# An attention block on one core: a transposed tile ahead of the whole score tile, and VectorE instead of ScalarE copying the V bank

## The chip, the cores and the metric

The kernel runs on one core of one Trainium2 chip. The core's engines work on their own instruction queues and wait for one another through semaphores: TensorE (matmuls; in the profile PE, and PEld for its weight loads), VectorE (DVE), ScalarE (ACT), GpSimd (POOL) and SyncE (SP, which here issues transfers). Matmul results lie in eight PSUM banks of 128 partitions x 512 floats; TensorE writes them, VectorE and ScalarE read them.

The metric is the device time of one execution in microseconds: 1590.65 (median of 3 runs).

## What is computed

```python
def _A_ref(x, wqkv, wo):                      # 2048 rows, D = 512, H = 32 heads of 16
    qkv = (x @ wqkv).reshape(B, S, 3, H, Dh).transpose(2, 0, 3, 1, 4)
    q, k, v = qkv[0], qkv[1], qkv[2]
    scores = jnp.einsum("bhqd,bhkd->bhqk", q, k) * (Dh ** -0.5)
    p = _softmax(scores, axis=-1)
    o = jnp.einsum("bhqk,bhkd->bhqd", p, v)
    return o.transpose(0, 2, 1, 3).reshape(B, S, D) @ wo
...
xn = _layernorm(x, axis=-1)
s = _A_ref(xn, A_wqkv, A_wo)
g = _silu(_B_ref(xn, B_w1, B_b1, B_w2, B_b2))     # gelu MLP, 512 -> 1376 -> 512
return x + s * g
```

With 32 heads of 16 columns each, there are 32 x 2048 x 2048 = 134 million scores, and as many exponentials.

## The kernel before, in words

The work falls into a first part (layer norm, the projections, the MLP, with score maxima mixed in), a long attention stage, and a tail that multiplies with `wo`, applies the gate and stores. The change touches the attention stage.

**Units and steps.** Four heads (a group `g`) and 512 queries (`c`) make a unit `u`; there are `NU` = 32 units. A unit takes 16 steps, one for each 128 keys. The loop over steps is in lines 966 to 984, and what a step issues, in which order, is a string of letters in `ORDER` (line 40):

- `T` (`t_one`, line 732): a transposed score tile, 128 keys x 512 queries of one head, one matmul (line 739) into a bank, and on ScalarE the exponential of it into SBUF (line 741). Four per step, one per head. The first two are on row side 1 of the matmul array (partitions 64 and up), the last two on row side 0. Four banks go round (`t_tile`, line 724), so a T takes the bank of the T four before it, and must wait for that one's exponential.
- `S` (line 210): a score tile the other way round, 128 queries x 512 keys, only for the row maximum that the softmax subtracts: one matmul (line 183) and on VectorE one `tensor_reduce` (line 189). The first S of a step is on row side 0, the second on side 1. This runs ahead of the T by up to `LEAD` = 144 steps.
- `X` and `Y` (lines 216 to 232): 256 keys of one head on side 0 and the same 256 keys of another head on side 1, in the two halves of one bank, with one reduce after Y. A step thus has three reduces. The S, X and Y tiles use three banks in a ring (`s_ring`). By the order in which the ring gives them out, the first S of a step takes the bank of the first S of the step before, X that of the second S, and the second S that of the X and Y.
- `V` (`pv_step`, line 798): the products with V for the step before, four matmuls in four column tiles into the one V bank, accumulated over a unit's 16 steps. (The trace shows each as two, so a V group has eight rows.) After a unit's last step the bank is copied into `OS[u]` (line 811), after which the next unit's first V matmul may overwrite it.

While score tiles remain to be made, a step is `ORDER[3]`; after step 490 it is `ORDER[0]`, without S, X and Y. Steps 0 and 1 have strings of their own (line 970).

**What hangs on the letters.** Between the T there are slots for other work (`todo`, filled by `at`, line 919): after the i-th T of a step the entries of position i are issued. Position 0 holds `o_move` (line 821: transfers on SP that read `OS[u]`) and `o_den` (line 830: a `reciprocal` on VectorE, then two transfers on SP); all else has position 3. When a unit's score tiles are complete, `s_end0` (line 238) puts one more reduce on VectorE (line 247) behind the next tile's reduce, and for each pair of units a transposing matmul (line 267) and a small copy follow the V of a later step.

Each engine executes its queue in the order of the program; nothing is rescheduled (`manual_schedule`). Two matmuls that stand next to each other on different row sides run side by side.

Of the kernel before, what the change touches and what calls it, by code (L numbers as in the profile page):

```python
# [10 lines left out]
AF = mybir.ActivationFunctionType  # L11
# [25 lines left out]
FILL0 = 30  # L37
HB = 4
W2B = 2
ORDER = {0: "TTTTV", 3: "STXTTSTYV"}  # L40
HC = CH // 2
PAIRED = 28
KB = 3
# [5 lines left out]
def fused(ctx: ExitStack, tc: tile.TileContext, x, wqk, wv, wo, w1, b1, w2, b2, out):  # L49
    nc = tc.nc  # L50
# [746 lines left out]
    PV, OS, DN, DR = {}, {}, {}, {}  # L797
    def pv_step(u, k):
        g = u // NCH
        if k == 0:  # L800
            PV[u] = ps_v.tile([P, CH], F32, name="pv")
        for j in range(GH):
            h = (g * GH + j) * VW
            nc.tensor.matmul(PV[u][32 * j:32 * j + 32, :], vsb[:, k, h:h + 32], PT[u, k][:, j, :],  # L804
                             start=(k == 0), stop=(k == NT - 1))
        del PT[u, k]
        if k == NT - 1:
            OS[u] = wb.tile([P, CH], F32, name="os", bufs=1)
            pv = PV.pop(u)
            if u < NU - 1:  # L810
                nc.scalar.activation(OS[u], pv, AF.Copy)
            else:
                nc.scalar.activation(OS[u][:, :HC], pv[:, :HC], AF.Copy)
                nc.vector.tensor_copy(OS[u][:, HC:], pv[:, HC:])
# [151 lines left out]
    for n in range(L + 1):  # L966
        ua, ka = divmod(n, 16)
        want = due(n) - due(n - 1)
        i = 0
        for op in ORDER[want] if n > 1 else ("TTTTV", "TTSTSVT")[n]:  # L970
            if op in "SXY":
                s_op(op)
            elif op == "V":
                if n:
                    pv_step(*divmod(n - 1, 16))
                for _ in range(4):
                    tick()
                flush()
            else:
                if EARLY <= 4 * n + i < 4 * L:  # L980
                    t_one(ua, ka, i % 2, 1 - i // 2)
                for f, args in todo.get((n, i), []):
                    f(*args)
                i += 1
# [54 lines left out]
```

## Time and profile before

| | us |
|---|---|
| median of 3 runs (1590.64 to 1590.91) | 1590.65 |
| the profiled execution | 1590.04 |
| its span, first to last instruction | 1588.3 |
| TensorE / VectorE / ScalarE busy in the span | 1581.8 / 1379.1 / 1259.1 |
| granted TensorE clock | 1.000 |

The attention stage takes from about 477 to 1499 us of the span. In the timeline, a row gives start, length, engine, line, operation, output and inputs, shape, and in brackets the idle time of the engine ahead of it with what ended it. Rows of one kind that follow one another on an engine are merged and counted with x. Several waits of one instruction are put down to the one that came last. TensorE's matmuls overlap and their ends are modelled, so the starts are what to read.

### The profile page before, as it was taken

The numbers are of one execution on the slowest core, as the hardware profiler recorded it, in microseconds if no ns is written. First come the engines' busy times: TensorE is split into PE (matmuls) and PEld (weight loads), VectorE is DVE, ScalarE is ACT, GpSimd is POOL, SyncE is SP. The second block draws the span as 40 slices with busy tenths as digits, with TensorE's granted clock in tenths as the row PEclk, the third lists the DMA queues.
The fourth block names the chain that finished last, engine by engine and source line by source line (L and its number), as shares of the span: only waits on it lengthen the run. The fifth ranks groups of instructions, "written<-read, shape, count | busy, mean of one in ns | idle before, by whom it ended". The sixth has DMA issues, their size and how long they took to land.

```text
span 1588.3 us, 31761 instructions
## 1 busy us (share of the span) xinstructions
PE 1581.8 (100%) x12144; PEld 934.7 (59%) x12144; DVE 1379.1 (87%) x2261; ACT 1259.1 (79%) x2520; POOL 373.7 (24%) x394
## 2 busy tenths in 40 slices
PE   9999999999999999999999999999999999999998
PEld 8899999999894444444444444444444444444445
DVE  7599898989889999999999999999999999999734
ACT  4334343434349999999999999999999999999984
POOL 4145575756640011001000100100100000000143
PEclk9999999999999999999999999999999999999999
DMA  6626343454332123112410511411150111110252
GB/s 206 150 59 161 109 137 99 157 139 134 114 96 59 37 42 59 28 38 47 76 31 25 70 41 30 62 39 29 33 76 21 32 29 36 36 29 22 59 192 101
DMA packets 74648, 116.87 MB, mean 74 GB/s; under 512 B 23012, under 2 KB 24292, under 8 KB 73320
## 3 DMA queue, kind: packets, MB, share of 16 engines
q1 hardware_dynamic: 70748, 101.89, 23.7%
q0 software_dynamic: 3264, 12.35, 4.5%
q8 instruction: 96, 1.57, 0.4%
q10 hardware_dynamic: 484, 0.60, 0.1%
q14 instruction: 56, 0.46, 0.1%
HBM read 84.35 MB, written 25.97 MB: 69 GB/s over the span
## 4 chain that ended last, share of the span: by engine, by line
PE 97%; ACT 1%; DVE 1%; issue 0%; DMA 0%; ACTq 0%; DVEq 0%
PE pv L804 33%; PE ps L183 24%; PE ps L590 12%; PE pst L739 10%; PE pst L590 7%; PE ps L739 3%; PE ps L80 3%; PE pv L590 2%; PE ps L458 1%; ACT slot L741 1%; PE pst L80 1%; DVE st L417 0%; PE pst L440 0%; DMA xt<-in_x 0%; PE pst L458 0%
## 5 line engine op out<-in xcount | busy, mean ns | idle before, releaser
L189 DVE TENSOR_REDUCE mx<-ps 128x2 f32<-128x512 f32 x2048 | 1299.5, 684 | 144.6 <-PE pst L739 35.2
L741 ACT ACTIVATE slot<-pst 128x512 f32<-128x512 f32 x1533 | 831.7, 614 | 17.8 <-PE pst L739 9.6
L804 PE MATMUL pv<-slot,vsb 128*32 128x512 f32 x4096 | 545.4, 605 | 0.0
L183 PEld LDWEIGHTS ps<-kt,slot 48*128 48x128 f32 x1364 | 223.8, 184 | 280.2 <-DVE mx L189 278.3
L183 PE MATMUL ps<-kt,slot 48*128 48x512 f32 x1364 | 379.4, 365 | 0.0
L739 PE MATMUL pst<-qt,kt 50*128 50x512 f32 x1149 | 376.0, 436 | 0.5 <-DVE gt L672 0.3
L741 ACT ACTIVATE slot<-ps 128x512 f32<-128x512 f32 x515 | 316.5, 615 | 2.5 <-PE ps L183 0.2
L590 PE MATMUL ps<-slot,w1h 64*128 64x512 f32 x1088 | 218.1, 393 | 0.0
L739 PEld LDWEIGHTS pst<-qt,kt 50*128 50x128 f32 x1149 | 188.6, 184 | 41.8 <-ACT slot L865 12.6
L183 PE MATMUL ps<-kt,qz 48*128 48x512 f32 x512 | 212.7, 415 | 0.0
L183 PEld LDWEIGHTS ps<-slot,slot 48*128 48x128 f32 x598 | 98.3, 184 | 121.5 <-DVE mx L189 120.7
L183 PE MATMUL ps<-slot,slot 48*128 48x512 f32 x598 | 166.0, 364 | 0.0
L739 PE MATMUL ps<-qt,kt 50*128 50x512 f32 x387 | 162.7, 422 | 0.0
L590 PEld LDWEIGHTS ps<-slot,w1h 64*128 64x128 f32 x1088 | 151.5, 185 | 8.4 <-ACT junk L604 2.6
L804 PEld LDWEIGHTS pv<-slot,vsb 128*32 128x32 f32 x4096 | 80.8, 108 | 109.2 <-issue 100.2
L590 PE MATMUL ps<-slot,w1l 64*128 64x512 f32 x544 | 141.9, 393 | 0.0
L377 POOL TENSOR_TENSOR hl<-hg,hh 128x512 fp32r<-128x512 f32 x76 | 96.8, 1295 | 129.7 <-ACT hh L376 85.9
L250 POOL CAST nmh<-nm 128x16 fp32r<-128x16 f32 x32 | 6.3, 196 | 477.4 <-DVE nm L247 409.3
L739 PE MATMUL pst<-qt,slot 50*128 50x512 f32 x384 | 113.4, 421 | 0.0
L604 ACT ACTIVATE junk<-ident_r 1x1 f32<-1x1 f32 x92 | 18.0, 196 | 116.5 <-PE pst L590 113.3
L183 PEld LDWEIGHTS ps<-kt,qz 48*128 48x128 f32 x512 | 93.8, 183 | 16.3
L842 POOL TENSOR_TENSOR ot<-ot,dn 64x512 f32<-64x512 f32 x15 | 19.6, 1304 | 299.7 <-DMA dn<-den_d 256.9
(159 smaller groups left out, 1757.7 us busy)
## 6 DMA issues: line engine op xcount, KB each, us to landing
raw<-in_w SPq DMA_DIRECT2D x88, 256.0 KB
qk_h<-hh SPq DMA_DIRECT2D x32, 256.0 KB
qk_l<-hl SPq DMA_DIRECT2D x32, 256.0 KB
qt<-qk_h SPq DMA_DIRECT2D x128, 64.0 KB
slot<-qk_h SPq DMA_DIRECT2D x92, 64.0 KB
g_d<-gt POOLq DMA_DIRECT2D x16, 256.0 KB, 3.5
qt<-qk_l SPq DMA_DIRECT2D x64, 64.0 KB
dn<-den_d SPq DMA_DIRECT2D x32, 128.0 KB
```

The costliest lines, as they stand in the source:

```text
L80: nc.tensor.matmul(ps, lhs[a], rhs[b], start=first and n == 0, stop=last and n == 2)
L183: return nc.tensor.matmul(ps[:, c0:c0 + w], QS[u][r, p, qi * P:(qi + 1) * P], kts[u // NCH % KB][p][r, k0:k0 + w], start=True, stop=True).ins
L189: nc.vector.tensor_reduce(MX[u][:, 2 * p:2 * p + 2, qi, ki][:, heads, parts], ps.rearrange("p (n c) -> p n c", c=HC), axis=AX.X, op=OP.max)
L250: nc.gpsimd.tensor_copy(hl[:, 0], nm)
L377: nc.gpsimd.tensor_sub(hl, raw, hh.bitcast(F32))
L458: nc.tensor.matmul(pq["q", g, c], W1[g][i][:, k * P:(k + 1) * P], (xh, xl)[j][c][:, k], start=n == 0 and k == 0, stop=n == 2 and k == KT - 1)
L590: i = nc.tensor.matmul(ps, lhs[r], rhs[r], start=first, stop=last).ins
L604: i = nc.scalar.activation(junk[:, :1], ident_r[:1, :1].bitcast(F32), AF.Copy).ins
L739: nc.tensor.matmul(ps, kts[g % KB][p][r, k * P:(k + 1) * P], QT[u][r, p, :], start=True, stop=True)
L741: nc.scalar.activation(PT[u, k][:, 2 * p + a, :], ps, AF.Exp, scale=SCALE)
L804: nc.tensor.matmul(PV[u][32 * j:32 * j + 32, :], vsb[:, k, h:h + 32], PT[u, k][:, j, :], start=(k == 0), stop=(k == NT - 1))
L842: eng.tensor_mul(ot[c][rs, g // 2], ot[c][rs, g // 2], DN.pop(u)[rs])
```

## The change

Two lines. The letter string of a full step begins with T instead of S, so that the first transposed tile stands ahead of the first whole score tile. And for all units but the last, the copy of the V bank is issued on VectorE instead of ScalarE.

```diff
-ORDER = {0: "TTTTV", 3: "STXTTSTYV"}
+ORDER = {0: "TTTTV", 3: "TSXTTSTYV"}
...
             if u < NU - 1:
-                nc.scalar.activation(OS[u], pv, AF.Copy)
+                nc.vector.tensor_copy(OS[u], pv)
             else:
```

In the built program, TensorE's queue has the two matmuls exchanged in each of these steps and no others moved; S still waits for VectorE alone and T for ScalarE. The unit's copy is gone from ScalarE's queue and stands on VectorE's behind the last reduce of the unit's last step. The reciprocal of `o_den` moves ahead of the first reduce of its step, since it follows the first T. The queues of GpSimd and SP are unchanged.

## The prediction

> **What bounds the kernel now.** I read the page first, then the busy time by stage.
>
> ```profile
> span 1588.3 us, 31761 instructions
> ...
> PE 97%; ACT 1%; DVE 1%; issue 0%; DMA 0%; ACTq 0%; DVEq 0%
> ```
> ```profile
> 577.81:777.70 199.89, 199.89 (x1540) 90.17 (x1539) 182.95 (x301) 197.98 (x391) 23.98 (x38) 1.00 0.27 50
> 500.00:1498.00 998.00, 998.00 (x7677) 450.06 (x7673) 913.26 (x1501) 988.11 (x1946) 74.59 (x123) 1.00 0.20 40
> 1498.00:1588.30 90.30, 86.27 (x477) 46.01 (x469) 37.03 (x53) 61.63 (x120) 36.26 (x28) 1.00 0.43 143
> ```
>
> The columns are PE, PEld, DVE, ACT, POOL, granted clock, DMA share, GB/s. The changed code runs in this long stage: 490 steps of four exponentials each, (2048 - 576) / 3 from the code. PE is full by its modelled ends, ACT 99%, DVE 92%. Such shares name no owner, so next I measured the step, on the chain of waits, and followed one step in the timeline.
>
> ```profile
> 767.40 1.07 PE pv L804 x8
> ...
> 775.61 1.07 PE pv L804 x8
> ```
> ```profile
> 563.95 0.68 DVE L189 TENSOR_REDUCE mx<-ps 128x2 f32<-128x512 f32 x1
> 564.30 0.50 PE L183 MATMUL ps<-slot,slot 48*128 48x512 f32 x1
> 564.31 0.49 PE L739 MATMUL pst<-qt,kt 50*128 50x512 f32 x1
> 564.87 1.58 ACT L741 ACTIVATE slot<-pst 128x512 f32<-128x512 f32 x3
> 565.32 1.07 PE L804 MATMUL pv<-slot,vsb 128*32 128x512 f32 x8
> 566.32 0.62 ACT L741 ACTIVATE slot<-ps 128x512 f32<-128x512 f32 x1
> 566.99 0.18 PEld L739 LDWEIGHTS ps<-qt,kt 50*128 50x128 f32 x1
> 567.42 0.64 PE L804 MATMUL pv<-slot,vsb 128*32 128x512 f32 x4
> ```
> ```profile
> 564.84 0.69 DVE L189 TENSOR_REDUCE mx<-ps 128x2 f32<-128x512 f32 x1 [0.21 <-PE ps L183]
> ```
> ```profile
> 568.42 0.49 PE L739 MATMUL pst<-qt,kt 50*128 50x512 f32 x1
> ```
>
> Each step ends with a V group. Four steps take 775.61 - 767.40 = 8.21 us, so two take 4.11. A ring of waits gives exactly that. The first T of a step (564.31) is answered by its exponential after 0.56 (564.87); the fourth exponential starts 1.45 later (566.32) and lasts 0.62; 0.05 after its end the fourth T of the *next* step, which needs that bank, loads its weights (566.99); the V group follows 0.43 later (567.42), and the next step's first T 1.00 after it (568.42). Sum 0.56 + 1.45 + 0.62 + 0.05 + 0.43 + 1.00 = 4.11. So the pace is a ring between TensorE and ScalarE over two steps.
>
> The second ring goes over VectorE:
>
> ```profile
> 561.49 1.22 DVE L189 TENSOR_REDUCE mx<-ps 128x2 f32<-128x512 f32 x2
> ```
> ```profile
> 562.76 0.18 PEld L183 LDWEIGHTS ps<-slot,slot 48*128 48x128 f32 x1
> 563.31 0.64 PE L804 MATMUL pv<-slot,vsb 128*32 128x512 f32 x4
> ```
> ```profile
> 608.38 1.89 DVE L189 TENSOR_REDUCE mx<-ps 128x2 f32<-128x512 f32 x3
> 610.47 1.89 DVE L189 TENSOR_REDUCE mx<-ps 128x2 f32<-128x512 f32 x3 [0.21 <-PE pst L739]
> 612.54 0.69 DVE L189 TENSOR_REDUCE mx<-ps 128x2 f32<-128x512 f32 x1 [0.18 <-PE pst L739]
> ```
>
> First S to its reduce 0.54 (564.30 to 564.84); three reduces 1.89; 0.05 from the third's end (562.71) to the weight load of the next step's second S (562.76); 0.55 from there to V; 1.00 to the next S: 4.03. It is 0.08 shorter than the first ring, and so does not show. TensorE alone can do 2.01, as in the step from 563.31 to 565.32, or 4.02 for two. One row misleads:
>
> ```profile
> PEld ps L183 <- DVE mx L189: 386.5, 461, 0.8
> ```
>
> TensorE's largest wait names VectorE. But the first S comes 1.00 after every V group, and T starts 0.01 after it: these 0.84 us are V's own streaming, during which no weights are loaded.
>
> **The swap of S and T.** Nothing is added; T starts 0.01 earlier at most. What differs is who is answered first. With S first, S's reduce starts 0.54 after S, T's exponential 0.56 to 0.57 after T. Before and behind the stage there are steps in which T comes first:
>
> ```profile
> 478.50 0.49 PE L739 MATMUL pst<-qt,kt 50*128 50x512 f32 x1
> ...
> 479.03 0.60 ACT L741 ACTIVATE slot<-pst 128x512 f32<-128x512 f32 x1 [0.83 <-PE ps L739]
> ```
> ```profile
> 1507.91 0.73 PE L739 MATMUL pst<-qt,kt 50*128 50x512 f32 x3
> ...
> 1508.45 1.57 ACT L741 ACTIVATE slot<-pst 128x512 f32<-128x512 f32 x3 [1.18 <-PE pst L739]
> ```
>
> There the exponential comes after 0.53 and 0.54. So the first of the pair is answered about 0.03 sooner, on either engine, and the second pays it. The swap takes 0.03 off the first ring (4.08) and puts 0.03 on the second (4.06); TensorE's own 4.02 lies below both. A unit of 16 steps has eight pairs; at its end the ring is broken by the stall described next, so seven or eight pairs count: 30.6 units x 7.5 x 0.03 = **6.9 us gained**. Bounds: 0, if T second is no cause, and 30.6 x 8 x 0.04 = 9.8, with 0.04 as the most that the rounded rows allow.
>
> The Trainium skill (TensorE: Matmul & The Clock Gate, "The cost: per-tile semaphore tail") says that the completion signals of matmuls running side by side are written one after another, 26.3 ns each. By that figure the term is an estimated 6.0 us, and the rule speaks against the swap as well: the delay isn't removed, S's reduces inherit it. The trace's 0.03 agrees.
>
> Two small things follow on VectorE. The reciprocal of line 832 is issued in the slot after the first T, so it now stands ahead of the step's first reduce, in idle time of 0.21, instead of between two reduces; and line 247's reduce finds a spare of 0.02 in the second ring where it found 0.08.
>
> ```profile
> L832 DVE RECIPROCAL dr<-dr 128x16 f32<-128x16 f32 x29 | 7.0, 242 | 0.0
> L247 DVE TENSOR_REDUCE nm<-mx 128x16 f32<-128x128 f32 x22 | 6.1, 275 | 0.0
> ```
>
> I take +0.02 x 29 = 0.6 gained (0 to 0.05 each) and 0.04 x 22 = 0.9 lost (0 to 0.06 each): **0.3 lost**. The SP and POOL queues keep their order; line 826's transfers wait for a copy that ends no later (below).
>
> **The copy.** Around a unit's end:
>
> ```profile
> 608.94 1.07 PE L804 MATMUL pv<-slot,vsb 128*32 128x512 f32 x8
> 609.93 0.50 PE L183 MATMUL ps<-kt,slot 48*128 48x512 f32 x1
> 610.33 0.63 ACT L811 ACTIVATE os<-pv 128x512 f32<-128x512 f32 x1
> 611.02 0.16 PEld L804 LDWEIGHTS pv<-slot,vsb 128*32 128x32 f32 x8 [0.23 <-ACT os L811]
> 612.24 0.69 ACT L741 ACTIVATE slot<-ps 128x512 f32<-128x512 f32 x1
> 612.98 0.18 PEld L739 LDWEIGHTS ps<-qt,kt 50*128 50x128 f32 x1 [0.30 <-ACT slot L741]
> 613.40 1.07 PE L804 MATMUL pv<-slot,vsb 128*32 128x512 f32 x8
> ```
>
> *Removed*: ScalarE's copy at 610.33 pushes the four exponentials back; the fourth ends 612.93, the T that needs its bank loads at 612.98, and the two steps take 613.40 - 608.94 = 4.46 instead of 4.11. That is 0.35 per unit, 10.5 us over the 30 units that end in this stage (a 31st ends behind it, where VectorE is busy 37 of 90 us, and I count nothing).
>
> *Added*: a copy on VectorE behind the third reduce of the unit's last step. No full copy of this bank on VectorE is in the trace; the nearest rows are its half and other readers of these banks:
>
> ```profile
> L814 DVE COPY os<-pv x1: 424/424/424, 1567.8 to 1567.8; 128x256 f32<-128x256 f32 x1
> L672 DVE TENSOR_TENSOR gt<-pv,b_sb x1: 692/692/692, 475.1 to 475.1; 128x512 f32<-128x512 f32 x1
> ```
>
> I take 0.69 long, and a slot of 0.60 in the queue, as the reduces have: (1.89 - 0.69) / 2. The third reduce starts at 608.38 + 2 x 0.60 = 609.58, with the swap 609.61. The copy runs from 610.21 (V ended at 610.01) to 610.90, and the V group, due at 609.93 + 1.02 = 610.95, finds its bank free; where steps are 0.05 shorter it is 0.05 late. Behind the copy wait the next three reduces: the first starts at 610.81 instead of 610.50, the third ends 612.70, the second S loads at 612.75, and V comes at 613.30 instead of 610.95 + 2.04 = 612.99. So VectorE stalls TensorE by 0.31 to 0.36 where ScalarE did by 0.35: nearly the whole gain is handed back. With 0.34 it is 30 x 0.01 = **0.3 us gained**. Ends: with 0.42, the half's length, as slot the stall is 0.16, gain 5.7; with a slot of 0.69, 0.43, loss 2.4.
>
> The Trainium skill (VectorE: DVE Perf Modes, "The DRAIN you can't avoid") holds that a VectorE instruction starts only when the pipe is empty, which gives the slot of 0.69. The reduces disagree: 0.60 from start to start though 0.69 long.
>
> **Sum.** 6.9 - 0.3 + 0.3 = 6.9 off the profiled execution's 1590.04 (its span 1588.3 and 1.7 around it): 1583.1. The median of the runs is 0.6 above that execution: **1583.8**.
>
> **The rivals.**
> - *The copy costs nothing.* If the slot is short and its lateness dies in VectorE's idle 0.21, the full 10.5 of the removed stall comes on top of the swap's: 1573.6. For it: VectorE is 92% busy. Against: the chain of 613.30 above. A partial case (slot 0.42) is 1578.4.
> - *The swap does nothing.* The two matmuls start 0.01 apart, and if 0.56 against 0.53 belongs to what surrounds those steps, only the copy's 0.3 is left: 1590.4, no change. For it: only steps of other make-up have T first. Against: S, when first, is answered after the same 0.54 on another engine.
> - *VectorE becomes the bound, and the kernel slower.* It decides once the first S's reduce starts 0.62 or more after S: then the second ring is 4.11 or longer. At 0.64 it is 4.13: 240 pairs x 0.02 = 4.8; line 247's slots come through, 22 x 0.08 = 1.8; each copy stalls 0.06 more than ScalarE's did, 1.8: 1599.0. For it: only 0.02 lies between the rings after the change. Against: the second of the pair is now answered within 0.57.
> - *The copy holds VectorE for its whole length*: 30 x 0.09 = 2.7 lost, 1586.5. Its basis is the page's rule above; the reduces speak against it.
>
> **How the numbers follow.** Forecast 0.50 (its own range 1580 to 1587.5); copy free or nearly 0.13; swap without effect 0.17; VectorE the bound 0.14; whole length 0.06. About 0.2% (3.2 us) is what a measurement of this kernel can tell from no change. Faster by more: 0.50 + 0.13 + 0.06, less 0.02 for the forecast's upper edge, 0.67; same 0.18; slower 0.15. The range takes in the forecast, the swap without effect, the partial copy and the whole length: 1576.5 to 1592.5.
>
> **What would show it.** Right: the first exponential 0.53 to 0.54 behind a step's first T, the first reduce 0.57 behind S; pairs of V groups 4.08 apart; at a unit's end a copy of some 0.69 on VectorE, then a V group about 0.3 late, with the second S's weight load 0.05 behind a reduce. Wrong: pairs still 4.11 apart (swap without effect), every second S loading 0.05 behind the third reduce (VectorE paces), or unit ends without a late V group.

## The result and the profile after

| | us |
|---|---|
| before, median of 6 runs beside it | 1590.64 |
| after, median of 6 runs (1580.57 to 1581.35) | 1580.92 |
| ratio, 95% interval | 0.9939, 0.9926 to 0.9952 |
| span of the profiled execution, before and after | 1588.3, 1579.0 |

The kernel became 9.7 us faster; 6.9 was forecast. Two lines of the page of the changed kernel, its span and the chain that ended last by engine, and TensorE's two longest waits between 500 and 1490 us (us in total, times, longest):

```profile
span 1579.0 us, 31736 instructions
...
PE 98%; DVE 1%; DMA 0%; issue 0%; ACT 0%; DVEq 0%
```
```profile
PEld pst L739 <- ACT slot L741: 295.5, 354, 0.8
PEld ps L739 <- ACT slot L741: 94.8, 113, 0.8
```

The chain by engine says as little as before. The two waits settle the row that the prediction called misleading. In the same stretch of the kernel before, 386.5 us were put down to VectorE, 0.84 us at each of 461 places. Now 295.5 + 94.8 = 390.3 us are put down to ScalarE, again 0.84 us at each of 467 places, because a T instead of an S is the first to load weights behind V. Only the name changed with the order, so it was a wait for neither engine.

Two steps of the changed kernel in the timeline, the later rows following the ring from a first T to the first T two steps on:

```profile
605.05 0.50 PE L739 MATMUL pst<-qt,kt 50*128 50x512 f32 x1
605.05 0.50 PE L183 MATMUL ps<-slot,slot 48*128 48x512 f32 x1
605.58 1.58 ACT L741 ACTIVATE slot<-pst 128x512 f32<-128x512 f32 x3
605.62 1.89 DVE L189 TENSOR_REDUCE mx<-ps 128x2 f32<-128x512 f32 x3 [0.18 <-PE ps L183]
607.03 0.62 ACT L741 ACTIVATE slot<-ps 128x512 f32<-128x512 f32 x1
```
```profile
607.70 0.18 PEld L739 LDWEIGHTS ps<-qt,kt 50*128 50x128 f32 x1
608.13 1.06 PE L804 MATMUL pv<-slot,vsb 128*32 128x512 f32 x8
609.12 0.50 PE L739 MATMUL pst<-qt,kt 50*128 50x512 f32 x1
```

The exponential now starts 0.53 behind T (605.58 - 605.05; before 0.56), the reduce 0.57 behind S (605.62 - 605.05; before 0.54). Over the steps away from the unit ends the medians say the same: 0.564 before and 0.533 now for the exponential, 0.535 and 0.565 for the reduce. The rest of the ring is as it was, 1.45, 0.62, 0.05 and 0.43, but for 0.99 instead of 1.00 at its end, since T no longer starts 0.01 behind S. Two steps take 609.12 - 605.05 = 4.07 where they took 4.11: 0.03 comes from the answer and 0.01 from the start.

The end of a unit, with the copy on VectorE:

```profile
608.13 1.06 PE L804 MATMUL pv<-slot,vsb 128*32 128x512 f32 x8
609.43 0.68 DVE L811 COPY os<-pv 128x512 f32<-128x512 f32 x1
610.03 2.47 DVE L189 TENSOR_REDUCE mx<-ps 128x2 f32<-128x512 f32 x4
610.17 0.16 PEld L804 LDWEIGHTS pv<-slot,vsb 128*32 128x32 f32 x8 [0.17 <-DVE os L811]
611.96 0.18 PEld L183 LDWEIGHTS ps<-kt,slot 48*128 48x128 f32 x1 [0.27 <-DVE mx L189]
612.51 1.06 PE L804 MATMUL pv<-slot,vsb 128*32 128x512 f32 x8
```

The copy lasts 0.68 and the next reduce starts 0.60 behind it. The third reduce from 610.03 ends 1.88 later, 611.91; the second S loads at 611.96, with the 0.27 now named; V follows 0.55 later. The two steps take 612.51 - 608.13 = 4.38, a stall of 0.31 over the ordinary 4.07. On average over the 30 units that end in the stage it is 4.40, a stall of 0.32.

### The profile page after: what moved, and what is told of

Same layout as the page of the kernel before. It is cut to its first block, busy times and chain, and to the rows that moved or that the text cites. A ratio compares the mean times of both kernels' runs of the same rounds, so it can differ in the third digit from the quotient of the medians.

```text
span 1579.0 us, 31736 instructions
## 1 busy us (share of the span) xinstructions
PE 1572.2 (100%) x12144; PEld 949.2 (60%) x12144; DVE 1396.2 (88%) x2292; ACT 1247.6 (79%) x2489; POOL 373.6 (24%) x394
## 4 chain that ended last, share of the span: by engine, by line
PE 98%; DVE 1%; DMA 0%; issue 0%; ACT 0%; DVEq 0%
PE pv L804 33%; PE pst L739 21%; PE ps L590 13%; PE ps L183 10%; PE pst L590 7%; PE ps L739 7%; PE ps L80 3%; PE pv L590 2%; PE ps L458 1%; PE pst L80 1%; DVE st L417 0%; PE pst L440 0%; DMA xt<-in_x 0%; PE pst L458 0%; DVE slot L75 0%; DVE xn L431 0%
## 5 line engine op out<-in xcount | busy, mean ns | idle before, releaser
L741 ACT ACTIVATE slot<-ps 128x512 f32<-128x512 f32 x515 | 311.2, 605 | 2.7 <-PE ps L183 1.8
L739 PEld LDWEIGHTS ps<-qt,kt 50*128 50x128 f32 x387 | 71.1, 184 | 42.1 <-ACT slot L741 36.4
```

The source lines that it names most:

```text
L739: nc.tensor.matmul(ps, kts[g % KB][p][r, k * P:(k + 1) * P], QT[u][r, p, :], start=True, stop=True)
L741: nc.scalar.activation(PT[u, k][:, 2 * p + a, :], ps, AF.Exp, scale=SCALE)
```

## The experiments

Every difference below is to runs of the kernel before on the same chip (1590.43 for the first four, 1589.85 for the last two). "The changed kernel" stands for its 9.7 below.

**The swap alone.**

```diff
-ORDER = {0: "TTTTV", 3: "STXTTSTYV"}
+ORDER = {0: "TTTTV", 3: "TSXTTSTYV"}
```

> T ahead of S in each full step, the V bank still copied by ScalarE. Two rings: the pair of steps goes from 4.11 to 4.07 or 4.08 us, the first exponential comes 0.53 behind the first T, the first reduce 0.57 behind S, and the stall of 0.35 at a unit's end stays. That is 30.6 units x 7 to 8 pairs x 0.035 = 7.5 to 8.5 us less than before, 1582 to 1583. Rival, the copy is what brought the time: at most 2 us less, and pairs of 4.11.

Measured 1583.72, 6.7 us less; ratio 0.9957 (0.9943 to 0.9970). That is 0.8 less gain than the least that was expected. Its V groups (an ordinary pair and the pair at a unit's end), ScalarE's rows in the latter, and the weight load that waits for them:

```profile
604.73 1.06 PE L804 MATMUL pv<-slot,vsb 128*32 128x512 f32 x8
...
608.80 1.07 PE L804 MATMUL pv<-slot,vsb 128*32 128x512 f32 x8
...
613.28 1.06 PE L804 MATMUL pv<-slot,vsb 128*32 128x512 f32 x8
```
```profile
608.29 1.57 ACT L741 ACTIVATE slot<-pst 128x512 f32<-128x512 f32 x3
609.74 0.62 ACT L741 ACTIVATE slot<-ps 128x512 f32<-128x512 f32 x1
610.22 0.63 ACT L811 ACTIVATE os<-pv 128x512 f32<-128x512 f32 x1
610.69 1.62 ACT L741 ACTIVATE slot<-pst 128x512 f32<-128x512 f32 x3
612.12 0.68 ACT L741 ACTIVATE slot<-ps 128x512 f32<-128x512 f32 x1
```
```profile
612.86 0.18 PEld L739 LDWEIGHTS ps<-qt,kt 50*128 50x128 f32 x1 [0.30 <-ACT slot L741]
```

The ordinary pair is 608.80 - 604.73 = 4.07, as forecast. But the pair with ScalarE's copy is 613.28 - 608.80 = 4.48, no shorter than the 4.46 of before. Over the 30 unit ends the average is 4.48 in both kernels. From 608.29 on, ScalarE's rows follow one another without idle time, the copy among them, so an earlier start of T is of no use there. The expectation had the stall unchanged at 0.35; measured against an ordinary pair of 4.07 it is 0.41.

So seven of a unit's eight pairs gain and the one at its end does not. From the V group at the end of the first unit to the one at the end of the thirtieth, the kernel before takes 967.6 us and this one 960.7: 6.9 less in 29 units, or 0.034 for each of seven pairs.

**The copy alone.**

```diff
-                nc.scalar.activation(OS[u], pv, AF.Copy)
+                nc.vector.tensor_copy(OS[u], pv)
```

> S ahead of T as before, the V bank copied by VectorE. Two rings: pairs stay at 4.11; at a unit's end VectorE's stall of 0.30 to 0.31 takes the place of ScalarE's 0.35: 30 x 0.045 = 1 to 2 us less than before, 1589 to 1590, and with the run of the swap alone it adds up to the 9.7 of the whole change. Rival, the copy is what brought the time: 8 us less or more. Rival, the two parts need each other: both alone bring less than 3.

Measured 1585.81, 4.6 us less; ratio 0.9971 (0.9959 to 0.9982): more than expected, less than the first rival says and more than the second allows. The V groups and the copy:

```profile
604.59 1.06 PE L804 MATMUL pv<-slot,vsb 128*32 128x512 f32 x8
...
608.70 1.06 PE L804 MATMUL pv<-slot,vsb 128*32 128x512 f32 x8
...
613.02 1.06 PE L804 MATMUL pv<-slot,vsb 128*32 128x512 f32 x8
```
```profile
609.95 0.68 DVE L811 COPY os<-pv 128x512 f32<-128x512 f32 x1
```

Ordinary pairs stay at 4.11. The pair at the unit's end is 4.32, a stall of 0.21 and not 0.31. The copy starts 609.95 - 608.70 = 1.25 behind the V group, where with the swap it starts 609.43 - 608.13 = 1.30 behind it; that S is answered 0.03 sooner when it comes first is a part of this, and the rest was not followed. The earlier copy makes most of the difference between 4.32 and 4.38; the other 0.04 of the stall is only that the ordinary pair is longer here. 30 x (0.35 - 0.21) = 4.2; over all 30 unit ends the average pair falls from 4.48 to 4.34.

The two parts alone sum to 11.3, together they bring 9.7. The unit ends show where the rest goes: on average the copy's move takes 4.48 to 4.34 without the swap, and only to 4.40 with it.

**One more small instruction on VectorE, ahead of the first reduce.** In this and the next run two lines are added near the top, so the page's line numbers are 2 higher there.

```diff
+    dmy = keep.tile([P, NT], F32, name="dmy")
+    nc.vector.memset(dmy, 1.0)
...
+        if want and n > 1:
+            nc.vector.reciprocal(dmy, dmy)
         for op in ORDER[want] if n > 1 else ("TTTTV", "TTSTSVT")[n]:
```

> The changed kernel with one more small VectorE instruction (a reciprocal of 128x16 on a scratch tile, a slot of 0.16 us) in each full step, at its start, ahead of the first reduce, where VectorE is idle for 0.2. Two rings: ordinary pairs stay at 4.07; only where VectorE has no idle time (behind a unit's copy, behind line 247's reduce) it shows: 30 x 0.16 + 22 x 0.1 = 5 to 8 us more than the changed kernel, 1586 to 1589. Rival, VectorE's amount of work sets the pace: 490 x 0.16 = 78 us more.

Measured 1583.84, 6.6 less than before and so 3.1 more than the changed kernel; ratio 0.9959 (0.9944 to 0.9973).

```profile
604.16 1.07 PE L806 MATMUL pv<-slot,vsb 128*32 128x512 f32 x8
...
608.23 1.06 PE L806 MATMUL pv<-slot,vsb 128*32 128x512 f32 x8
...
612.72 1.07 PE L806 MATMUL pv<-slot,vsb 128*32 128x512 f32 x8
```

The ordinary pair is 4.07 as without it; the pair at the unit's end is 4.49 instead of 4.38, 30 x 0.11 = 3.3. Some 490 instructions cost what 30 of them cost. The expectation had 5 to 8, because it took 0.16 for the slot (the time from an instruction's start to the next one's), where the next run shows that the instruction adds 0.10, and because it counted 22 x 0.1 for line 247's reduces, which do not show.

**The same instruction behind the first reduce.**

```diff
                 s_op(op)
+                if op == "S" and whole and n > 1:
+                    nc.vector.reciprocal(dmy, dmy)
```

> The same instruction in each full step, but behind the first reduce, between it and the second. Two rings: the ring over VectorE grows from 4.06 by 0.16 to 4.22 and takes over: 0.15 more for each of 245 pairs, some 35 us more than the changed kernel, about 1616, and the second S of each step loads 0.05 behind a reduce's end. Rival, the amount of work or idle time decides and not the place: the same time as the run with the instruction ahead of the first reduce, within 3 us.

Measured 1601.01, 10.6 more than before and 20.3 more than the changed kernel; ratio 1.0067 (1.0048 to 1.0085). The timeline's V groups, then VectorE's rows, then the second S's weight load:

```profile
563.71 1.07 PE L806 MATMUL pv<-slot,vsb 128*32 128x512 f32 x8
...
567.86 1.07 PE L806 MATMUL pv<-slot,vsb 128*32 128x512 f32 x8
```
```profile
565.27 0.69 DVE L191 TENSOR_REDUCE mx<-ps 128x2 f32<-128x512 f32 x1
```
```profile
565.88 0.24 DVE L976 RECIPROCAL dmy<-dmy 128x16 f32<-128x16 f32 x1
566.04 1.22 DVE L191 TENSOR_REDUCE mx<-ps 128x2 f32<-128x512 f32 x2
```
```profile
567.32 0.18 PEld L185 LDWEIGHTS ps<-slot,slot 48*128 48x128 f32 x1
```

The second S loads 0.06 behind the end of the third reduce (566.04 + 1.22 = 567.26): the ring over VectorE now paces, at 567.86 - 563.71 = 4.15 per pair. From the first reduce's start to the third's end it is 567.26 - 565.27 = 1.99 instead of 1.89, so the instruction really adds 0.10, since the reduce behind it takes a shorter slot. That makes the ring 4.05 without it: 0.02 below ScalarE's, as the prediction had it (4.06 to 4.08). The size was expected too large by that slot: the pair grew by 0.08 and not by 0.15, and 245 x 0.08 = 19.6. The place decides by a factor of 6 to 7, 20.3 against 3.1 for the same work.

**The second S last in the stalled step.** Of each unit one step, the second behind the copy, gets another order of letters.

```diff
-        for op in ORDER[want] if n > 1 else ("TTTTV", "TTSTSVT")[n]:
+        for op in "TSXTTYTSV" if want and n % 16 == 2 and n > 2 else ORDER[want] if n > 1 else ("TTTTV", "TTSTSVT")[n]:
```

> The changed kernel, with another order of letters, TSXTTYTSV, in one step of each unit: the second step behind the copy, whose second S waits for VectorE. There the second S goes last, and Y ahead of the fourth T. Two rings: the S still cannot start before the late reduce has ended, 0.90 behind the step's start, but only V is behind it, which then comes at about 1.23 instead of 1.34: 30 x 0.11 = 3.3 us less than the changed kernel, 1577 to 1578. Rival, V follows the second S by the same 0.44 wherever it stands, or Y's wait for X costs as much: no change within 1 us.

Measured 1577.70, 12.15 less than before; ratio 0.9920 (0.9907 to 0.9934); span 1575.9 against 1579.0.

```profile
607.79 1.06 PE L804 MATMUL pv<-slot,vsb 128*32 128x512 f32 x8
...
612.09 1.06 PE L804 MATMUL pv<-slot,vsb 128*32 128x512 f32 x8
```
```profile
610.87 0.50 PE L739 MATMUL pst<-qt,kt 50*128 50x512 f32 x1
...
611.66 0.18 PEld L183 LDWEIGHTS ps<-kt,slot 48*128 48x128 f32 x1
```

V comes 612.09 - 610.87 = 1.22 behind the step's start, 1.23 was expected, and 0.43 behind the S's load instead of 0.55. The pair is 4.30 instead of 4.38, and over the 30 unit ends 4.29 instead of 4.40 on average: 30 x 0.11 = 3.3. By the medians it is 2.4 us better than the changed kernel, by the spans 3.1; the intervals of the two ratios overlap, the timeline does not leave it in doubt. It is the fastest version here that computes the whole.

**No copy at all.**

```diff
-                nc.vector.tensor_copy(OS[u], pv)
+                nc.gpsimd.memset(OS[u], 1.0)
```

> The changed kernel without the copy of the V bank for all units but the last: GpSimd fills the copy's place with ones, so the output leaves the attention values of these units out. It measures what a copy costs at all. Two rings: the whole stall at a unit's end goes, 30 x 0.31 = 9.4 us less than the changed kernel, about 1571.5, which is 12.2 less than the run of the swap alone, or 0.40 per copy on ScalarE. Rival, most of the copy is hidden in idle time of VectorE: at most 3 us less.

Measured 1572.20, 17.65 less than before; ratio 0.9887 (0.9874 to 0.9901). That is 7.9 us below the changed kernel (8.4 by the spans) and 10.9 below the swap alone, 0.26 (0.28) and 0.36 per copy, where 0.31 and 0.40 were expected. The rival, hidden for the most part, is out. What is missing shows next to it:

```profile
607.27 1.06 PE L804 MATMUL pv<-slot,vsb 128*32 128x512 f32 x8
...
611.34 1.06 PE L804 MATMUL pv<-slot,vsb 128*32 128x512 f32 x8
...
613.56 1.07 PE L804 MATMUL pv<-slot,vsb 128*32 128x512 f32 x8
```
```profile
611.49 0.28 DVE L247 TENSOR_REDUCE nm<-mx 128x16 f32<-128x128 f32 x1
```

The unit's end is an ordinary 4.07, as at all 30 unit ends. But here the step behind it takes 2.22, with line 247's reduce between two reduces and no late step for it to hide in; in the changed kernel that reduce starts in the late step itself (612.42), and the step from 612.51 on takes 2.01 (its next V group is at 614.52). That reduce falls behind 7 of the 30 unit ends, and the step there is about 0.17 longer than an ordinary one: some 1.2 us in all, which is what the spans' 8.4 is short of 30 x 0.32 = 9.6.

## Why the prediction was right, and where its sizes were off

*Forecast and range.* 1580.92 lies in the range and in the forecast's own range; the direction and the mechanism were right.

*What bounds the kernel.* The ring over ScalarE was the pace and is still: 4.11, then 4.07. The second ring, over VectorE, was put at 4.06; the run with the instruction behind the first reduce gives 4.05. The shares of busy time would have said otherwise: VectorE at 92% took 490 more instructions for 3 us in one place and for 20 in the other.

*The swap.* Forecast 6.9; alone it brought 6.7. The 0.03 was right, and it is paid by S as forecast. That the figure fits so well is partly luck: 7.5 pairs of a unit were counted at 0.03. The ordinary pair in fact shrank by 0.04, as T's start also moved by the 0.01 that the prediction named and did not count, and only seven pairs gain, 0.034 each on average: the one at the unit's end does not.

*The copy.* This is the mis-sized term: "30 x 0.01 = 0.3 us gained". Measured on top of the swap it is 9.7 - 6.7 = 3.0 by the medians, and 30 x (0.41 - 0.32) = 2.7 by the average stalls of the two traces. Two numbers behind it were off. VectorE's stall was taken at 0.34 out of 0.31 to 0.36 and is 0.32 on average. And ScalarE's stall was taken as 0.35, one unit's 4.46 over pairs of 4.11; with the swap it is 0.41, on average 4.48 over pairs of 4.07, because the late end does not move when the ordinary pairs get shorter. The copy itself was right: 0.68 long (0.69), slot 0.60, the second S loading 0.05 behind the third reduce, V 0.55 after that.

*The small terms*, 0.6 for the reciprocal and 0.9 for line 247, were not measured by themselves.

*The rivals.* "The swap does nothing" falls with the swap alone. "The copy costs nothing" falls with the stall in the timeline and the run without a copy. Its partial case (slot 0.42, 1578.4) falls with the slot of 0.60, though the time alone, 1580.92, lies about halfway between it and the forecast of 1583.8. "VectorE becomes the bound" did not happen, but was near: the run behind the first reduce is that rival made real, with 0.10 more in its ring, and it was slower than before. "The copy holds VectorE for its whole length" falls with 609.43 to 610.03: 0.60 from start to start. The prediction gave the Trainium skill's rule (VectorE: DVE Perf Modes, "The DRAIN you can't avoid") without its exception: the same section says that a next instruction which is not held starts earlier. The 0.60 after a copy 0.68 long agrees with the exception.

*Left open.* Why the second of two matmuls that run side by side is answered later. The Trainium skill's 26.3 ns per completion signal (TensorE: Matmul & The Clock Gate, "The cost: per-tile semaphore tail") is near the 0.03 us seen, but no run took a signal away.

## What to carry to other kernels

Where queues run in order and buffers are few, look for rings: add up the waits from one instruction to the same one some iterations later, over each engine, and compare the sums. An instruction costs by the ring it falls into and by its place in it, not by its engine's share of busy time. When two changes meet, price the second in the kernel that has the first: a stall is a difference to the ordinary step, and grows when the ordinary step shrinks.

## What the hardware showed that was not expected

- A reduce between the small reciprocal and another reduce takes a shorter slot than one between two reduces: the two reduces from 566.04 span 1.22, the last of them lasts 0.68, so the first's slot is 0.54 instead of 0.60. A reciprocal of 0.24 between two reduces, with a slot of 0.16, therefore adds only 0.10 to the chain.
- Taking away one stall uncovered another of about 0.17 in the step behind it, at the 7 of 30 unit ends where line 247's reduce follows, so the copies' removal brought 0.04 to 0.05 per copy less than their stall in the trace.
